# The second MoE's row blocks of one expert, taken two at a time through one split of the weights

## The chip, the cores and the metric

The program runs on one core of one Trainium2 chip. The metric is the device time of one execution in microseconds (us). The kernel before took 2382.6 us, the median of three runs from 2382.53 to 2384.66.

## The reference

An attention with a threshold on its scores feeds a dense mixture of experts (all 8 experts for every row, weighted by a gate that is normalised eight times over rows and columns). Its output x, 2304 rows of 512, goes into a second mixture in which each row is computed by one expert only. The change touches this last part alone:

```
logits = x @ w_gate
expert_idx = np.argmax(logits, axis=1)
...
gate_w = probs[np.arange(N), expert_idx]
for e in range(E):
    mask = expert_idx == e
    if not mask.any():
        continue
    xe = x[mask]
    h = np.maximum(xe @ w1[e], 0.0)
    ye = h @ w2[e]
    out[mask] = gate_w[mask, None] * ye
```

There are 8 experts; w1 is 512 x 1024 and w2 is 1024 x 512 for each.

## The kernel before

**Numbers in two halves.** Every large product is made with operands that are split into a rounded high half and a low half (the number less its high half). High by high, high by low and low by high give three products on TensorE in place of one. A split is a rounding copy, mostly on ScalarE, followed by a subtraction on VectorE or GpSimd (POOL in the profile).

**The stages.** Attention comes first, then the first MoE, whose first product is in line 567 and whose second is in line 583. When its last expert is done with two tiles of rows, these are routed: gate logits, the arg max, the probability, and the rank of each row within its expert. The second MoE, function `moe2`, follows.

**Slots.** The rows of one expert are cut into blocks of 128, and each block is a slot. The table function turns the counts per expert into a list of slots (expert, first rank), finds the rows of each slot by a small product (`ids`, line 1094) and the gate values (`gat`). This is done two times: after 14 of the 18 tiles, for the first KE = 6 slots, which take blocks that are already full, and after all tiles for the others. The first NU = 24 slots always run; the 25th runs in a branch if rows are left for it. The list is interleaved, so that the even slots walk through the experts in order, and the odd slots do the same.

**One slot.** Its 128 rows are gathered by an indirect DMA of POOL (`gath`, line 1150), transposed (`tx`, line 1156) and split. The expert's weights come in eight pieces of 128 x 1024: four of w1 (j = 0 to 3) and four of w2 (j = 4 to 7). Each piece is loaded by SyncE's queue (SP, line 1144) into a raw buffer, `xall` for even slots and `accs` for odd ones, and only if the expert differs from that of two slots before; otherwise the raw piece is still there. The split is done anew for every slot: the high half in line 1168 (`wsh`), the low half in line 1172 (`wsl`), into one of nine tiles `w` that go around as a ring. The first product (`g1`, line 1180) holds the rows stationary and moves the weights, 24 products of 512 columns into two banks. A ReLU (line 1187) takes the hidden rows to SBUF, eight transposes turn them (`th`, line 1192), lines 1197 and 1201 split them, and the second product (`g2`, line 1210) is again 24 products of 512 columns. ScalarE scales by the gate (`ys`, line 1216), and POOL scatters the rows to the output (line 1219).

**What sets the order.** Every engine works its instructions in the order in which they were written. That order comes from a list scheduler at build time (class `Sched`): each step is given an engine, a duration in us, a due time and the steps it needs, and resources that it takes and gives back (eight PSUM banks "b", nine weight tiles "w", and small pools "hh", "xs", "wr"). A slot's due time is `U0 + 1 + 2 * s`; a weight piece's place in the order of use is `pos(s, j)`, and its split is due 1.1 before that, its load 5 before. The second table's steps are put into the same plan, due at `U0 - 1.5`.

Of the kernel before, what the change touches and what calls it, by code (L numbers as in the profile page):

```python
# [10 lines left out]
F32 = mybir.dt.float32  # L11
# [11 lines left out]
class Sched:  # L23
# [18 lines left out]
    def run(self):  # L42
# [9 lines left out]
        ready = {e: [] for e in engs}      # (prio, i, ready_time)  # L52
# [6 lines left out]
        relq = []                          # (time, seq, op, own engine)  # L59
# [42 lines left out]
class Ring:  # L102
    """tiles handed out in the order in which they were given back"""
# [13 lines left out]
def attention(tc, sc, cst, dram, xT, q, k, v, tau, also=None):  # L117
# [11 lines left out]
    with ExitStack() as ctx:  # L129
        # first the tiles that the last pair is done with early: what comes after takes their place  # L130
# [190 lines left out]
        # the sums' reciprocals, from one per partition to one per column: turned, then spread over the partitions through DRAM  # L321
# [190 lines left out]
def moe1(tc, sc, cst, pools, xT, acc, wgs, w1, w2, NE=8, NW=9):  # L512
# [19 lines left out]
    # the first pieces are split by the engines that the attention leaves first  # L532
# [195 lines left out]
def out_row(i, hf):  # L728
    """first output row and row step of half tile hf of column tile i"""
# [3 lines left out]
TG = 2          # tiles routed together  # L733
TE = 14         # tiles that give the first slots
KE = 6          # slots that their full blocks fill
NU = 24         # slots that always run; the others run if rows are left for them


def moe2_setup(tc, cst, one, dram, w_gates, E=8, N=2304, NS=25):
    """constants and tables that no data goes into"""  # L740
# [37 lines left out]
def moe2_iota(tc, cst, r, E=8, NT=18, NS=25):  # L778
    nc = tc.nc
    nc.gpsimd.affine_select(out=r["lt"], in_=cst["ones"], pattern=[[1, 128]], compare_op=ALU.is_gt, fill=0.0, base=0, channel_multiplier=-1)  # L780
    nc.gpsimd.affine_select(out=r["tri"], in_=cst["ones"][:, 0:E * E].rearrange("p (a b) -> p a b", a=E), pattern=[[1, E], [-1, E]],
# [5 lines left out]
    # the blocks, in the order of their experts, go to the even slots first and then to the odd ones  # L787
    c = 128 + 2 * E
    for s0, n in ((0, KE // 2), (KE, (NU - KE) // 2)):
        nc.gpsimd.iota(it[:, c + s0:c + s0 + 2 * n].rearrange("p (a b) -> p a b", b=2), pattern=[[1, n], [n, 2]], base=0, channel_multiplier=0)  # L790
    nc.gpsimd.iota(it[:, c + NU:c + NS], pattern=[[1, NS - NU]], base=NU - KE, channel_multiplier=0)
    for i in range(NT):
        for hf in range(2):
            b, st = out_row(i, hf)
            c = 128 + 2 * E + NS + i
# [14 lines left out]
def moe2(tc, sc, cst, mt, pools, xall, accs, acc, w1, w2, out, elast, NS=25):  # L810
# [165 lines left out]
    def ohq(i):  # L976
        if i == 0:
            T["q"] = xs_p.tile([128, NT, 128], BF16, name="ohq", tag="xs")
# [43 lines left out]

# [1 line left out]
    ci = one.tile([128, 2, E], I32, name="ci")  # L1024
    cf = one.tile([128, 8, E], F32, name="cf")
    pr = one.tile([128, E, E], F32, name="pr")
    ge = one.tile([128, 2, NS, E], F32, name="ge")
    sl = one.tile([128, 4, NS], F32, name="sl")
    tab = one.tile([1, 2, NS], I32, name="tab")
    more = one.tile([1, 1], I32, name="more")  # L1030
    idi = one.tile([128, NS], I32, name="idi")
    idv = one.tile([128, 5, NS], F32, name="idv")
    gat = one.tile([128, NS], F32, name="gat")
    eq = one.tile([128, NT, NS - KE], BF16, name="eq")
    rhs = one.tile([128, NT, 5 * (NS - KE)], BF16, name="rhs")
    ful, cum, exc, ear, rem, dd = (cf[:, n] for n in range(6))
    erow, code, srow, tmp = (sl[:, n] for n in range(4))
    V_ = nc.vector

    def table(w, s0, s1, tiles, addc):  # L1040
        """the operations that make slots s0..s1 from the rows of the first `tiles` tiles, in order"""
        n = s1 - s0
        bs = lambda ap: ap.unsqueeze(1).to_broadcast([128, n, E])
        G0, G1 = ge[:, 0, 0:n], ge[:, 1, 0:n]
        it = mt["perm"][:, s0:s1]
        fin = w == 1
# [4 lines left out]
        L = [(P, .2, cnt, ["h"], []),  # L1051
             (V, .1, lambda: V_.tensor_scalar(ci[:, 0], T.pop(("cnt", w))[:, 0:E], addc, None, op0=ALU.add), [], ["h"]),
             (V, .1, lambda: V_.tensor_scalar(ci[:, 1], ci[:, 0], 7, None, op0=ALU.arith_shift_right), [], []),
             (V, .1, lambda: V_.tensor_copy(rem if fin else ful, ci[:, 1]), [], [])]
# [304 lines left out]
```

## Time and profile before

| what | value |
|---|---|
| median of 3 runs | 2382.6 us |
| span of the profiled execution | 2381.7 us |
| TensorE, matmuls (PE) | 2297.8 us busy, 96% |
| TensorE, weight loads (PEld) | 2052.2 us, 86% |
| VectorE (DVE) | 1059.0 us, 44% |
| ScalarE (ACT) | 824.0 us, 35% |
| GpSimd (POOL) | 828.3 us, 35% |
| first MoE, 400 to 1900 us | PE 1498.8 of 1500 us busy, DVE 322.3, ACT 312.4, POOL 317.1 |
| second MoE, 1987 to 2375 us | PE 332.2 of 388 us busy, DVE 366.1, ACT 216.2, POOL 244.6, granted clock 0.95 |

Shares over the whole span hide the stages. The second MoE is about a sixth of the time, and there VectorE is busy for 94% of the stretch, whereas it is busy for 21% of the first MoE's. A busy TensorE in such a table is not TensorE at its peak: a product that runs at a lower clock is counted as busy for longer. Engines other than TensorE cost time only where TensorE waits for them.

### The profile page before, as it was taken

Reading aid. Unit: us, or ns where it says so; the run is one execution under the profiler, and the core shown is the slowest. Engines: PE = TensorE matmul, PEld = TensorE weight load, DVE = VectorE, ACT = ScalarE, POOL = GpSimd, SP = SyncE. Lnnn points to the kernel's source line nnn. Section 1 sums busy time; section 2 is a strip of 40 time slices with the busy share of each in tenths; the row PEclk is TensorE's granted clock in tenths of the full one; section 3 lists DMA queues with packets and bytes.
Section 4 is the critical chain, followed back from the end, with each engine's and each line's share of the span. In section 5 each row is a group of like instructions: output and inputs, shape, how many; then the busy total and the mean of one; then the engine's idle time right before and its main releaser. Section 6 shows DMA issues by size and latency. Waiting matters only on the chain.

```text
span 2381.7 us, 32447 instructions
## 1 busy us (share of the span) xinstructions
PE 2297.8 (96%) x12379; PEld 2052.2 (86%) x12379; DVE 1059.0 (44%) x1944; ACT 824.0 (35%) x1466; POOL 828.3 (35%) x713
## 2 busy tenths in 40 slices
PE   7999999999999999999999999999999998788897
PEld 7999988888999999999999999999998887676675
DVE  8999972114221112211121112211122348999997
ACT  6888852122113112211211311221122124455564
POOL 6777752023214103211411401231041004566665
PEclk9999999999999999999999999999999999999999
DMA  3222120001002001100200200010011016343442
GB/s 91 61 62 62 38 92 28 1 18 54 1 1 71 1 1 36 36 1 1 71 1 1 65 7 1 18 54 1 1 36 27 14 45 256 107 154 116 170 153 86
DMA packets 98445, 121.25 MB, mean 51 GB/s; under 512 B 18830, under 2 KB 64030, under 8 KB 98272
## 3 DMA queue, kind: packets, MB, share of 16 engines
q1 hardware_dynamic: 94368, 109.71, 14.2%
q0 software_dynamic: 3920, 9.45, 1.1%
q8 instruction: 98, 1.61, 0.3%
q14 instruction: 59, 0.48, 0.1%
HBM read 164.92 MB, written 13.18 MB: 75 GB/s over the span
## 4 chain that ended last, share of the span: by engine, by line
PE 81%; DVE 10%; issue 4%; DMA 2%; ACT 2%; POOL 1%; SPq 0%; POOLq 0%; ACTq 0%; DVEq 0%
PE h L567 34%; PE y L583 33%; DVE w L1172 6%; PE pt_av L407 4%; PE s L282 3%; PE pt_m L350 2%; PE sy L1210 1%; DVE w L1168 1%; ACT w L1168 1%; DMA xall<-in_moe_w_dram 1%; POOL w L1172 1%; PE pt_k L251 1%; DVE hst L1201 1%; PE pt_av L410 1%; PE pt_q L241 0%
## 5 line engine op out<-in xcount | busy, mean ns | idle before, releaser
L567 PE MATMUL h<-xs,w 128*128 128x384 f32 x4608 | 871.1, 337 | 1.8 <-ACT w L539 1.0
L583 PE MATMUL y<-w,hh 128*128 128x512 f32 x3456 | 868.4, 395 | 3.7 <-ACT hh L572 2.3
L567 PEld LDWEIGHTS h<-xs,w 128*128 128x128 f32 x4608 | 819.1, 188 | 35.6 <-ACT w L539 1.4
L576 DVE SCALAR_TENSOR_TENSOR hh<-h,hh 128x384 fp32r<-128x384 f32 x384 | 214.2, 558 | 1211.3 <-ACT hh L572 1211.3
L583 PEld LDWEIGHTS y<-w,hh 128*128 128x128 f32 x3456 | 642.0, 188 | 120.6 <-ACT hh L572 2.8
L572 ACT ACTIVATE hh<-h 128x384 fp32r<-128x384 f32 x384 | 188.8, 492 | 1175.6 <-PE h L567 1153.0
L560 POOL TENSOR_TENSOR xs<-xall,xs 128x384 fp32r<-128x384 f32 x192 | 189.3, 1020 | 1114.6 <-ACT xs L539 1114.6
L1210 PE MATMUL sy<-w,hst 128*128 128x512 f32 x576 | 162.1, 427 | 42.7 <-DVE w L1172 40.2
L1210 PEld LDWEIGHTS sy<-w,hst 128*128 128x128 f32 x576 | 114.9, 204 | 76.0 <-DVE w L1172 48.6
L551 POOL TENSOR_TENSOR w<-wr,w 128x1024 fp32r<-128x1024 f32 x57 | 136.7, 2399 | 116.7 <-ACT w L539 113.2
L1180 PE MATMUL sh<-w,xst 128*128 128x512 f32 x576 | 150.7, 406 | 8.3 <-DVE w L1172 5.6
L407 PE MATMUL pt_av<-PTh,vsp 128*128 128x288 f32 x512 | 144.4, 323 | 0.0
L1180 PEld LDWEIGHTS sh<-w,xst 128*128 128x128 f32 x576 | 107.3, 193 | 38.0 <-DVE w L1172 12.1
L1172 DVE TENSOR_TENSOR w<-acc,w 128x1024 fp32r<-128x1024 f32 x60 | 128.6, 2155 | 10.8 <-ACT w L1168 10.4
L1172 DVE TENSOR_TENSOR w<-xall,w 128x1024 fp32r<-128x1024 f32 x60 | 127.5, 2136 | 9.2 <-ACT w L1168 8.9
L304 ACT ACTIVATE p<-s,stat 128x576 f32<-128x576 f32 x144 | 108.1, 752 | 30.7 <-DVE stat L287 30.5
L310 DVE SCALAR_TENSOR_TENSOR p<-s,stat,p 128x576 f32<-128x576 f32 x144 | 116.1, 809 | 4.9 <-ACT p L304 2.2
L287 DVE TENSOR_REDUCE stat<-s 128x1 f32<-128x576 f32 x144 | 108.2, 753 | 13.5 <-PE s L282 13.4
L282 PE MATMUL s<-kk,qst 128*128 128x288 f32 x512 | 96.7, 313 | 2.0 <-DVE p L310 1.8
L1172 POOL TENSOR_TENSOR w<-acc,w 128x1024 fp32r<-128x1024 f32 x36 | 92.8, 2584 | 16.5 <-ACT w L1168 15.7
L539 ACT CAST w<-wr 128x1024 fp32r<-128x1024 f32 x63 | 66.0, 1049 | 90.1 <-PE y L583 85.6
L1172 POOL TENSOR_TENSOR w<-xall,w 128x1024 fp32r<-128x1024 f32 x36 | 89.5, 2494 | 13.6 <-ACT w L1168 12.9
(222 smaller groups left out, 2079.1 us busy)
## 6 DMA issues: line engine op xcount, KB each, us to landing
xall<-in_moe_w_dram SPq DMA_DIRECT2D x104, 512.0 KB
acc<-in_moe_w_dram SPq DMA_DIRECT2D x96, 512.0 KB
wr<-in_moe_w_dram SPq DMA_DIRECT2D x128, 256.0 KB
kr<-in_k_dram SPq DMA_DIRECT2D x16, 256.0 KB
qr<-in_q_dram SPq DMA_DIRECT2D x16, 256.0 KB
vr<-in_v_dram SPq DMA_DIRECT2D x16, 256.0 KB
rbc<-rd SPq DMA_DIRECT2D x32, 128.0 KB
x1d<-acc SPq DMA_DIRECT2D x28, 128.0 KB
```

What stands on the lines that cost most here:

```text
L282: nc.tensor.matmul(ps[:, half, 0:288], lh, kk[p][:, h, s, half * 288:(half + 1) * 288], start=(i == 0 and s == 0), stop=(i == len(parts) - ...
L310: nc.vector.scalar_tensor_tensor(t, stile.pop(g)[:, :, 0:288], s[:, 1, j:j + 1], t, op0=ALU.is_ge, op1=ALU.mult, accum_out=s[:, 2, j:j + 1])
L407: nc.tensor.matmul(ps[:, 0:288], vv[:, h * 4 + kc, i, 64 - 64 * h:192 - 64 * h], mv[:, h, kc, c0:c1], start=(h == 0 and kc == 0 and n == 0 ...
L551: (nc.vector if WL(e, f) == V else nc.gpsimd).tensor_tensor(t[:, 1], wr[e, f], t[:, 0].bitcast(F32), op=ALU.subtract)
L560: nc.gpsimd.tensor_tensor(t[:, 1, k], xT[k][:, c * CH:(c + 1) * CH], t[:, 0, k].bitcast(F32), op=ALU.subtract)
L567: nc.tensor.matmul(ps[:, 0:CH], w[:, i, k * 128:(k + 1) * 128], x[:, j, k], start=(k == 0 and i + j == 0), stop=(k == NK - 1 and i == 1))
L572: nc.scalar.activation(hh[e, c, f][:, 0], hps[e, c, f][:, 0:CH], AF.Relu)
L576: nc.vector.scalar_tensor_tensor(t[:, 1], hps.pop((e, c, f))[:, 0:CH], 0.0, t[:, 0].bitcast(F32), op0=ALU.max, op1=ALU.subtract)
L583: nc.tensor.matmul(yps[e, c, t], h[:, i, t * 128:(t + 1) * 128], w[:, j, 512:1024], start=(f == 0 and i + j == 0), stop=(f == NF - 1 and i ...
L1172: eng.tensor_tensor(t[:, 1], rawp(s, j), t[:, 0].bitcast(F32), op=ALU.subtract)
L1180: nc.tensor.matmul(T["h", s][hf], x[:, i, k * 128:(k + 1) * 128], w[:, j, hf * 512:(hf + 1) * 512], start=(k == 0 and i + j == 0), stop=(k ...
L1210: nc.tensor.matmul(T["y", s], h[:, i, f * 128:(f + 1) * 128], w[:, j, r * 512:(r + 1) * 512], start=(f == 0 and i + j == 0), stop=(f == 7 ...
```

## The change

**Units in place of slots.** The list now has units. A pair is 256 rows of one expert, a single is 128. Three pairs come from the early table (KP = 3), then seven pairs (NP = 7) and four singles (NS = 4) always run, in the order MAIN, in which a single stands after each of the pairs with the numbers 4 to 7. Five more pairs (NR = 5, the units REST) run in a branch if rows are left for them.

```
+TG = 2
+TE = 14
+KP = 3
+NP = 7
+NS = 4
+NR = 5
+MAIN = [0, 1, 2, 3, 4, 10, 5, 11, 6, 12, 7, 13, 8, 9]
...
+def half(s, h):
...
+    return 2 * s + h - max(0, min(s - KP - NP, NS))
```

**Weights.** Each unit, pair or single, loads and splits its eight pieces once, and the load no longer depends on the expert of the unit before. All high halves are ScalarE's (six of eight were), all low halves VectorE's (five of eight were, the pieces 1, 4 and 7 were POOL's).

```
     def ld_w(s, j):
-        nc.sync.dma_start(out=rawv(s, j), in_=wsrc(j, bass.ds(T["e", s], 1)), cond=(T["c", s] != 0), cond_hint=False)
+        nc.sync.dma_start(out=rawv(s, j), in_=wsrc(j, bass.ds(T["e", s], 1)))
...
-    def wsl(s, j, eng):
+        nc.scalar.copy(T["w", s, j][:, 0], rawp(s, j))
+
+    def wsl(s, j):
         t = T["w", s, j]
-        eng.tensor_tensor(t[:, 1], rawp(s, j), t[:, 0].bitcast(F32), op=ALU.subtract)
+        nc.vector.tensor_tensor(t[:, 1], rawp(s, j), t[:, 0].bitcast(F32), op=ALU.subtract)
```

**A pair's products.** Two gathers and two sets of transposes fill one tile of 4 x 256 columns. In the first product (`q1`) the weights are held and the rows move: 256 columns a product, 96 products a pair, into four banks. The hidden values come out turned already, so `prh` (ReLU and rounding, ScalarE) and `prl` (ReLU and subtraction, VectorE) split them straight from PSUM, and no transposes follow. The second product (`q2`) is 48 products of 512 columns, 24 for each half of the rows. Singles keep `g1`, `th` and `g2`.

```
+    def q1(s, k, b):
+        if k == 0:
+            T["hp", s, b] = bank(f"hp{s}_{b}")
+        x, w, ps = T["xs", s], T["w", s, k], T["hp", s, b]
+        for r in range(2):
+            f = 2 * b + r
+            for i, j in SPL:
+                nc.tensor.matmul(ps[:, r * 256:(r + 1) * 256], w[:, i, f * 128:(f + 1) * 128], x[:, j, k * 256:(k + 1) * 256],
+                                 start=(k + r + i + j == 0), stop=(k == 3 and i == 1), skip_group_check=True)
...
+    def prl(s, b):
+        t = T["hh", s, b]
+        nc.vector.scalar_tensor_tensor(t[:, 1], T.pop(("hp", s, b)), 0.0, t[:, 0].bitcast(F32), op0=ALU.max, op1=ALU.subtract)
+
+    def q2(s, b, r, h):
...
+        t, w = T["hh", s, b], T["w", s, 4 + b]
+        c = r * 256 + h * 128
+        for i, j in SPL:
+            nc.tensor.matmul(T["y", s, h], t[:, i, c:c + 128], w[:, j, r * 512:(r + 1) * 512],
+                             start=(b + r + i + j == 0), stop=(b == 3 and r == 1 and i == 1))
```

**The plan.** A unit's place is `at[s]`, which grows by 2 for a single and 4 for a pair; as before, a piece is loaded when the unit two places earlier in the order has split its own.

```
-        """place of a weight piece in the order of use, 4 to a phase of 5 us"""
-        return U0 + 1 + 2 * s + .25 * j if j < 4 else U0 + 4 + 2 * s + .25 * (j - 4)
+        n = len(hs_of(s))
+        return at[s] + .25 * n * j
...
-            op(("wh2", s, j), V if hi_v else A, .6 if hi_v else .95, pu - 1.1, partial(wsh, s, j, hi_v), [("rwin", s, j), ("wh2",) + prevp if prevp else first], acq=["w"])
-            op(("wl2", s, j), G if lo_g else V, 2.36 if lo_g else 1.13, pu - 1.1, partial(wsl, s, j, nc.gpsimd if lo_g else nc.vector), [("wh2", s, j)])
+            op(("wh2", s, j), A, 1.05, pu - 1.1, partial(wsh, s, j), [("rwin", s, j), ("wh2",) + prevp if prevp else first], acq=["w"])
+            op(("wl2", s, j), V, 1.25, pu - 1.1, partial(wsl, s, j), [("wh2", s, j)])
```

**The tables** deal out pairs first and singles behind them; the comparison of every row with every slot (`EQ`, and the five products `R` of it) grows in the second table from 18 x 19 to 18 x 28 elements a partition, and is written into the tile `ohq`, which the pool "xs" gets back after the index product.

**The order on VectorE around the second table.** Before, the bulk operations of the table (line 1098) stood between the roundings and subtractions of two slots. `w` is a weight tile of the ring, `hst3` the split hidden rows of slot 3, `rhs` the table's operand:

```order
L1085 CAST tab_5095<-sl_5094 1x19
L1097 TENSOR_TENSOR eq_5100<-sl_5094,gf_5088 128x342
L1098 TENSOR_TENSOR rhs_5101<-eq_5100,idp_82 128x18x19
L1172 TENSOR_TENSOR w4_5062<-xall_69,w4_5062 128x1024
L1098 TENSOR_TENSOR rhs_5101<-eq_5100,idp_82 128x18x19
L1168 CAST w5_5063<-xall_69 128x1024
L1098 TENSOR_TENSOR rhs_5101<-eq_5100,gp_5086 128x18x19
L1201 TENSOR_TENSOR hst3_17266<-th3_0_17130,hst3_17266 128x512
```

Now they stand together, and behind the index products (`ids1`) four subtractions of the fourth unit's weights (line 1227, out of the raw buffer `acc`) come ahead of the third pair's first hidden half (`hp2_0`, line 1250):

```order
L1146 TENSOR_TENSOR ohq_16181<-ohq_16181,gp_5086 128x18x28 x3
L1227 TENSOR_TENSOR w0_5058<-acc0_5067,w0_5058 128x1024
L1150 COPY idv_5100<-ids1_17250 128x5x28
L1151 SCALAR_TENSOR_TENSOR idt_5099<-idv_5100 128x28
L1152 TENSOR_SCALAR idt_5099<-idt_5099 128x28
L1153 SCALAR_TENSOR_TENSOR idi_5098<-idt_5099 128x28
L1154 TENSOR_TENSOR gat_5101<-idv_5100 128x28
L1227 TENSOR_TENSOR w6_5064<-acc1_5068,w6_5064 128x1024
L1155 TENSOR_TENSOR gat_5101<-gat_5101,idv_5100 128x28
L1227 TENSOR_TENSOR w7_5065<-acc2_5069,w7_5065 128x1024
L1227 TENSOR_TENSOR w2_5060<-acc3_5070,w2_5060 128x1024
L1250 SCALAR_TENSOR_TENSOR hp2_0_17346<-hp2_0_17138,hp2_0_17346 128x512
```

In line 1250's row the destination and the first operand are the tile of the hidden half and the PSUM bank, both called `hp2_0`.

**The order on TensorE.** Before, in the middle of the stage, one slot's second product (`sy8`) filled the time in which the next slot's hidden rows were rounded and turned (`th9`):

```order
L1180 MATMUL sh9_1_18106<-w1_5059,xst9_18033 128x512
L1210 MATMUL sy8_18160<-w7_5065,hst8_18083 128x512 x6
L1210 MATMUL sy8_18160<-w0_5058,hst8_18083 128x512 x6
L1192 MATMUL th9_0_18181<-ident_62,hr9_18167 128x128 x4
L1192 MATMUL th9_1_18187<-ident_62,hr9_18167 128x128 x4
L1210 MATMUL sy8_18160<-w3_5061,hst8_18083 128x512 x6
```

Now a single (unit 10) has the next pair's first products (`hp5`) at that place:

```order
L1270 MATMUL sh10_1_17958<-w6_5064,xst10_17924 128x512
L1239 MATMUL hp5_0_18025<-xst5_18004,w4_5062 128x256 x6
L1282 MATMUL th10_0_18033<-ident_62,hr10_18022 128x128 x4
L1239 MATMUL hp5_1_18039<-xst5_18004,w4_5062 128x256 x6
L1282 MATMUL th10_1_18050<-ident_62,hr10_18022 128x128 x4
L1239 MATMUL hp5_2_18055<-xst5_18004,w4_5062 128x256 x6
L1239 MATMUL hp5_3_18065<-xst5_18004,w4_5062 128x256 x6
L1300 MATMUL sy10_18073<-w7_5065,hst10_18048 128x512 x6
```

Between the two products of a pair (here unit 4, `hp4` and `py4`) stands only the transposing of the next unit's rows, where a slot before had its own transposes:

```order
L1239 MATMUL hp4_2_17773<-xst4_17679,w7_5065 128x256 x6
L1239 MATMUL hp4_3_17781<-xst4_17679,w7_5065 128x256 x6
L1208 MATMUL tx10_0_17877<-ident_62,xall_69 128x128 x4
L1258 MATMUL py4_0_17884<-w2_5060,hp4_0_17856 128x512 x3
L1258 MATMUL py4_1_17892<-w2_5060,hp4_0_17856 128x512 x3
```

So the banks `hp4_0` to `hp4_3` are filled in the order in which the second product takes them, and the first of them is complete three groups of six before the last.

More of the change, by code (lines that the diff above doesn't have):

```diff
@@ L1031, in moe2 @@
[L1031 to L1037, printed above, removed]
-    V_ = nc.vector
[L1040 to L1044, printed above, removed]
+    ci = one.tile([128, 2, 2 * E], I32, name="ci")
@@ new lines, in moe2, with table @@
+    gat = one.tile([128, NH], F32, name="gat")
+    num, cum, exc, dd, vv, bb = (cf[:, n] for n in range(6))
+    ear = cf[:, 6, 0:E]
+    mm = cf[:, 7, 0:1]
+    erow, code, srow, unit = (sl[:, n] for n in range(4))
+    V_ = nc.vector
+    def table(w):
+        s0, s1 = (KP, NT_) if w else (0, KP)
+        h0, h1 = (2 * KP, NH) if w else (0, 2 * KP)
+        S = 2 * E if w else E
+        tiles = NT if w else TE
+        n, m = s1 - s0, h1 - h0
+        bs = lambda ap: ap[:, 0:S].unsqueeze(1).to_broadcast([128, n, S])
+        G0, G1 = ge[:, 0, 0:n, 0:S], ge[:, 1, 0:n, 0:S]
@@ L1107, in table @@
-        return L, nreg
+                nc.tensor.matmul(ps[:, 0:5 * m], T["q"][:, i], T["rhs"][:, i, 0:5 * m], start=(i == 0), stop=(i == tiles - 1))
+        neq = len(L)
+        big = .06 + .00105 * tiles * m
+        v(lambda: V_.tensor_tensor(EQ(), ch[:, h0:h1].unsqueeze(1).to_broadcast([128, tiles, m]), b2(gf), op=ALU.is_equal), big)
+        for a in range(5):
+            v(lambda a=a: V_.tensor_tensor(R()[:, :, a], EQ(), b2(mt["idp"][:, a] if a < 2 else gp[:, a - 2]), op=ALU.mult), big)
@@ L1223, in moe2 @@
     xdone = [("xl", elast, 5, k) for k in range(4)] + [("xh", elast, 5, k) for k in range(4)]
+    order = MAIN + REST
+    turn = {s: n for n, s in enumerate(order)}
+    hs_of = lambda s: range(1 if single(s) else 2)
+    at, u = {}, U0 + 1
+    for s in order:
+        at[s] = u
+        u += 2 * len(hs_of(s))
+    uend = at[REST[0]]
     for i in range(2):
@@ L1275, in moe2 @@
-    splits(op, range(NU), ("lg1", TE // TG - 1))
-    for s in range(NU):
+        u = at[s]
+        one_ = single(s)
+        for h in hs_of(s):
+            op(("tx", s, h), P, .44, u - 1.6, partial(tx, s, h), [("gain", s, h)], acq=["b"])
+            op(("txh", s, h), A, .6, u - 1.6, partial(txh, s, h), [("tx", s, h)] + ([("txh", s, 0)] if h else []), acq=["hh" if one_ else "xs"] if h == 0 else [])
+            op(("txl", s, h), V, .6, u - 1.6, partial(txl, s, h), [("txh", s, h)], rel=["b"])
@@ L1277, in moe2 @@
+        for h in hs_of(s):
+            op(("ys", s, h), A, .7, u + 1, partial(ys, s, h), [last[h]], acq=["wr"], rel=["b"])
+            op(("sca", s, h), G, 1.2, u + 1, partial(scao, s, h), [("ys", s, h)])
+            op(("scao", s, h), "DMA", .8, u + 3.3, lambda: None, [("sca", s, h)], rel=["wr"])
+    splits(op, MAIN, ("lg1", TE // TG - 1))
+    for s in MAIN:
+        loads(op, s)
         slot(op, s)
@@ L1288, in rest @@
                 s2.res(nm, n)
-            splits(s2.op, range(NU, NS), None)
-            for s in range(NU, NS):
+            splits(s2.op, REST, None)
+            for s in REST:
+                loads(s2.op, s)
                 slot(s2.op, s)
```

320 lines of the change are left out of this document (188 added, 132 removed).

## The prediction

> **What bounds the kernel now.** I read the windows first, to find the stage that the change touches, then who waits for whom in it, then the groups of instructions, and last the timeline of one stretch. The second MoE's slots run from about 1987 us to the end. A window from the middle of them, with its columns (stretch, length, busy us of PE, PEld, DVE, ACT, POOL, the granted clock, DMA share, GB/s):
>
> ```profile
> 2180.00:2240.00 60.00, 51.21 (x234) 40.34 (x232) 57.76 (x38) 36.40 (x48) 41.24 (x20) 0.97 0.56 195
> ```
>
> VectorE is busy for 57.8 of 60 us there, ScalarE for 36.4, and the DMA engines for 56%. TensorE's 51.2 also counts slowed products. What TensorE waited for from 1950 us on (total, times, longest):
>
> ```profile
> PE sy L1210 <- DVE w L1172: 40.2, 24, 3.9
> PE sh L1180 <- DVE w L1172: 5.6, 8, 1.6
> ```
>
> The wait is for one line, the low half of a weight piece. The groups (count, then busy us and mean ns):
>
> ```profile
> L1172 DVE TENSOR_TENSOR w<-acc,w 128x1024 fp32r<-128x1024 f32 x60 | 128.6, 2155 | 10.8 <-ACT w L1168 10.4
> L1172 DVE TENSOR_TENSOR w<-xall,w 128x1024 fp32r<-128x1024 f32 x60 | 127.5, 2136 | 9.2 <-ACT w L1168 8.9
> L1172 POOL TENSOR_TENSOR w<-acc,w 128x1024 fp32r<-128x1024 f32 x36 | 92.8, 2584 | 16.5 <-ACT w L1168 15.7
> L1168 ACT CAST w<-acc 128x1024 fp32r<-128x1024 f32 x72 | 74.1, 1050 | 3.4 <-DMA acc<-in_moe_w_dram 3.4
> L1201 DVE TENSOR_TENSOR hst<-th,hst 128x512 fp32r<-128x512 f32 x48 | 32.5, 680 | 0.5 <-ACT hst L1197 0.5
> L1150 POOL DMA_INDIRECT xall<-x1d,idi x25 | 39.2, 1567 | 82.1 <-DVE gat L1106 62.5 <-PE tx L1156 16.0 <-issue 2.2
> ```
>
> A subtraction means 2.15 us on VectorE. The timeline shows why (start, length, engine):
>
> ```profile
> 2324.93 1.23 DVE L1172 TENSOR_TENSOR w<-acc,w 128x1024 fp32r<-128x1024 f32 x1
> ...
> 2325.83 2.60 POOL L1172 TENSOR_TENSOR w<-xall,w 128x1024 fp32r<-128x1024 f32 x1
> 2326.08 3.43 DVE L1172 TENSOR_TENSOR w<-xall,w 128x1024 fp32r<-128x1024 f32 x1
> ```
>
> Alone it takes 1.23 us; begun under POOL's subtraction it ends 1.1 us after that one (2329.51 against 2328.43). It stood still until POOL was done. So GpSimd's share of the split costs VectorE about what it saves, and VectorE (5 subtractions at 2.15, two roundings, three 0.68s: 14.6 us a slot) sets the pace above TensorE's own work.
>
> **TensorE's own work.** Back-to-back rates from the chain of waits in stretches where TensorE never stops (start, length, count):
>
> ```profile
> 1905.17 2.10 PE h L567 x12
> 1907.27 2.08 PE y L583 x9
> 1913.54 1.75 PE x1t L857 x16
> 1918.09 0.91 PE l1t L875 x8
> ```
> ```profile
> 150.08 0.64 PE pt_k L251 x8
> 160.86 1.60 PE pt_av L407 x12
> ```
>
> That is 0.231 us for a product of 512 columns, 0.175 for 384, 0.133 for 288, 0.114 for 256 with 16 columns of weights, 0.080 for 128, and 0.109 for an fp32 transpose. A slot has 48 products of 512 and 12 transposes: 11.09 + 1.31 = 12.4 us, and 24 slots 297.6 us. The stage lasts from
>
> ```profile
> 1987.26 0.60 PE L1156 MATMUL tx<-ident,xall 128*128 128x128 f32 x4
> ```
> to the end of
> ```profile
> 2372.74 1.43 PE L1210 MATMUL sy<-w,hst 128*128 128x512 f32 x5 [0.40 <-POOL w L1172]
> ```
>
> 386.9 us. Routing and tables inside it take about 6.0 (16 transposes 1.75, two gate groups 1.82, the rest an estimate from rows of their kind). So **386.9 - 297.6 - 6.0 = 83.3 us are lost**: 46 are the two waits above, some 7 are smaller ones, and about 30 are products at a reduced clock, as here after a wait:
>
> ```profile
> 2080.00:2084.00 4.00, 0.61 (x2) 0.51 (x3) 4.00 (x2) 0.91 (x2) 2.25 (x1) 0.85 0.95 341
> 2084.00:2088.00 4.00, 4.00 (x11) 3.14 (x10) 3.96 (x6) 0.00 (x0) 0.00 (x0) 0.50 0.99 380
> ```
>
> The Trainium skill's page "TensorE: Matmul & The Clock Gate" (section "HAM oscillation — how this bites in real kernels") says that idle gaps beyond some 3.4 us bring the half clock back. The 0.50 after a window that was nearly all idle agrees; by that rule the 30 us go as soon as no wait is that long, and if they stayed, the sum below would be 2328.
>
> **The change, part by part.** Counting rows per expert in the reference (292, 134, 1263, 394, 46, 1, 18, 156) gives 24 blocks before. With 1792 rows known early, three full pairs of one expert exist; seven pairs and four single blocks are left, exactly what always runs. So there are 10 pairs and 4 singles.
>
> *First product.* In a pair it is 96 products of 256 columns with 128 columns of weights, a form that the trace does not show. It lies between 0.114 (same width, fewer weight columns) and 0.133 (wider); a line through the 128 and 288 rows gives 0.122, which I take. Pair: 96 x 0.122 + 48 x 0.231 + 8 x 0.109 = 23.7 us against 24.8 for two slots; the hidden rows' transposes go. In all 236.7 + 49.6 = 286.3 us: **-11.3**, with bounds -19 and -1.
>
> The same page (section "LDWEIGHTS (loading the stationary operand)") gives columns/1.2, so 107 ns for 128 columns. By it the load still fits under 256 columns; unhidden, 960 products would cost 103 us more, and the sum would be 2400. The 128-column row at 0.080, below 107, speaks against the figure.
>
> *Splits.* 14 units have 112 pieces instead of 192, each 1.05 us of ScalarE and one subtraction of VectorE. The two prices of a subtraction with POOL elsewhere are the 1.23 above and this row of the chain, which counts from one start to the next:
>
> ```profile
> 2009.80 1.13 DVE w L1172
> ```
>
> I take 1.13 to 1.23, since POOL keeps only indirect DMAs; the other end is 2.15. A pair needs VectorE for 8 x 1.13 + 6 x 0.65 = 13 us of 23.7, a single for 8 x 1.13 + 3 x 0.65 = 11 of 12.4; ScalarE needs 8 x 1.05 for the pieces, 0.6 for each of a pair's six and a single's five other roundings, and 0.7 for each scaled output: 13.4 and 12.1. Singles stand between pairs, so each cycle of 36.1 us holds 24 of VectorE and 25.5 of ScalarE, and the nine weight tiles let the splits run eight pieces ahead. With this cover the 83.3 us go; at 2.15 a cycle needs 40 us of VectorE, and four cycles lose 16.
>
> *Loads.* Every unit loads its 4.2 MB: 14 loads, where the slots' experts by the same count made 12. A busy window moved
>
> ```profile
> 1988.00:1992.00 4.00, 4.00 (x27) 3.52 (x26) 3.70 (x4) 3.37 (x6) 3.42 (x2) 1.00 1.04 398
> ```
> 398 GB/s, so a unit takes 10.5 us, under each 12.4 or 23.7. Two raw buffers give a load a whole unit of time. Cost 0, except once, next.
>
> *The second table.* It grows to some 45 small operations (about 0.18 each), and its bulk ones from 342 to 504 elements:
>
> ```profile
> 2055.92 0.50 DVE L1098 TENSOR_TENSOR rhs<-eq,gp 128x342 bf16<-128x342 bf16 x1
> ```
> so 0.67 each. From the first pair's product to the index products VectorE has 20 subtractions (22.6), 16 half-size subtractions (10), 87 small ones (15.7), 9 bulk ones (5.3) and 1.1 of comparisons: 54.7 us. TensorE comes there after two pairs (47.4), routing (2.6) and nine groups of six (6.6): 56.6 us after its first product at 1989.1, at 2045.7. I take 1 us of wait (bounds 0 and 10, a quarter of the small ones' gaps). Behind it VectorE's order puts the fourth unit's first four subtractions ahead of the third pair's hidden halves (hp2), and that unit's loads wait for the table. What a table cost the first time:
>
> ```profile
> 1970.32 0.16 DVE L1085 CAST tab<-sl 1x6 int32<-1x6 f32 x1
> ...
> 1976.85 1.05 ACT L1168 CAST w<-xall 128x1024 fp32r<-128x1024 f32 x1 [3.36 <-DMA xall<-in_moe_w_dram]
> ...
> 1980.48 1.04 ACT L1168 CAST w<-xall 128x1024 fp32r<-128x1024 f32 x1 [0.39 <-DMA xall<-in_moe_w_dram]
> ```
>
> 6.4 us from the table to the first rounding, then 3.6 for two more pieces. The table stands at about 2041, so the fourth piece is subtracted at about 2054.6 and the first hidden half done at 2055.5; TensorE wants it at 2052.6. **3 us** (bounds 0 and 12). With 0.7 at the first pair, the early waits are 4.7.
>
> *Within units.* From a pair's first to its second product stands a ReLU rounding of 512 columns, like this group, and a subtraction like L1201's (0.68):
>
> ```profile
> L1187 ACT ACTIVATE hr<-sh 128x512 f32<-128x512 f32 x48 | 28.4, 598 | 39.9 <-PE sh L1180 39.9
> ```
>
> Together 1.3 us. The first bank is done three groups of six (2.2 us) before the last, so I take 0.2 us a pair for what else may be late, an estimate: 2.0 in all. In a single, roundings of the next pair's pieces stand between the two ReLUs: 0.6 each, 2.4. At the end a second scatter follows: 0.5.
>
> **Sum:** -11.3 - 83.3 + 4.7 + 2.0 + 2.4 + 0.5 = **-85.0**. It is made against the profiled execution:
>
> ```profile
> span 2381.7 us, 32447 instructions
> ```
>
> The median run, 2382.6, is 0.9 above that: 2296.7 of span, **2297.6** of time.
>
> **Rivals.** (1) The waits are 15 to 30 us larger: the table chain is in order on a VectorE with 2 us to spare, and each late operation delays the index products, the gathers and the loads behind them: 2312 to 2328. For it stands a row of the same view of waits, at the index products:
>
> ```profile
> PE ids L1094 <- DVE rhs L1098: 2.3, 1, 2.3
> ```
>
> Against it: POOL no longer stops VectorE. (2) VectorE still stands still under POOL's DMA work (mean 1567 ns a gather): 16 + 20 early subtractions x 1 us = 36, 2333; here the change would not do what it says. Against it, this subtraction kept its 1.22 us while a scatter was issued (timeline):
>
> ```profile
> 2048.14 1.22 DVE L1172 TENSOR_TENSOR w<-xall,w 128x1024 fp32r<-128x1024 f32 x1
> 2048.41 1.84 POOL L1219 DMA_INDIRECT out_dram<-ys,idi  x1 [0.67 <-DVE tab L1080]
> ```
> (3) The first product is paced by its weight loads at the length in their records,
>
> ```profile
> L567 PEld LDWEIGHTS h<-xs,w 128*128 128x128 f32 x4608 | 819.1, 188 | 35.6 <-ACT w L539 1.4
> ```
> 188 ns: 960 x 0.066 = 63, 2361. Against it, that same load ran under 0.175 and, in the 128 rows, 0.080. (4) Slower than before: a fifth single block or an eighth late pair. Then the branch runs five more pairs, 5 x 23.7 = 118, and their first load cannot start before it (6.4 and a gather): about 2425. It decides at one block; 134 rows of one expert are 6 above a block's edge, 394 of another 10.
>
> **How the numbers follow.** The forecast with its bounds, 2282 to 2312: 0.70. Rival 1: 0.15. Rival 2: 0.05. Rival 3: 0.06. Rival 4: 0.03. Below 2282: 0.01. The range runs to rival 1's end, 2282 to 2328, 0.85. A measurement here tells about 0.2% (4.8 us) from no change. Faster by more: 0.96, the same 0.01, slower 0.03.
>
> **What would show it.** Right: L1227 on VectorE at about 1.2 us with 112 executed, no subtraction on POOL in this stage, a group of six 256-column products at 0.73, a pair and a single in 36 us, TensorE over 95% busy at clock 1.0 after 2070, waits for the stage near 9 us, 24 scatters, last product near 2289. Wrong: L1227 near 2 us (rival 2), groups of six at 0.8 or more (rival 3), a gap of over 10 us at the index products or at the fourth unit (rival 1), more than 24 scatters (rival 4). A queue that I took as covered, such as roundings that wait for a weight tile while ReLUs stand behind them on ScalarE, would show as waits of every unit, not of one.

## The result and the profile after

| | before | after |
|---|---|---|
| median time | 2382.57 us (2382.01 to 2384.66, 4 runs) | 2293.61 us (2292.15 to 2293.86, 4 runs) |
| span of the profiled execution | 2381.7 us | 2290.4 us |

The ratio is 0.9619, with a 95% interval from 0.9606 to 0.9633: 89.0 us less, where 85.0 were forecast. The page of after, its first line and the busy times of the engines (us, share of the span, instructions):

```profile
span 2290.4 us, 31977 instructions
PE 2254.2 (98%) x12699; PEld 2048.7 (89%) x12699; DVE 887.6 (39%) x1904; ACT 780.0 (34%) x1394; POOL 634.5 (28%) x641
```

Two windows of after, the stretch of the early pairs and that of the pairs and singles behind them (columns as in the prediction):

```profile
1985.00:2045.00 60.00, 59.76 (x423) 54.69 (x422) 51.77 (x140) 33.15 (x46) 8.09 (x7) 1.00 0.65 236
2085.00:2275.00 190.00, 190.00 (x1150) 169.35 (x1150) 117.79 (x120) 114.50 (x143) 32.97 (x28) 1.00 0.58 190
```

TensorE is now busy for 190 of 190 us at the full clock, and VectorE for 62%. In the window from the middle of before it was 51 of 60, with VectorE at 96%. The groups show the subtraction alone with VectorE, and the new product with its weight load (count, busy us, mean ns, idle before):

```profile
L1227 DVE TENSOR_TENSOR w<-acc,w 128x1024 fp32r<-128x1024 f32 x56 | 68.4, 1223 | 36.3 <-ACT w L1223 35.5
L1227 DVE TENSOR_TENSOR w<-xall,w 128x1024 fp32r<-128x1024 f32 x56 | 67.8, 1223 | 30.0 <-ACT w L1223 29.2
L1239 PE MATMUL hp<-xst,w 128*128 128x256 f32 x960 | 121.6, 284 | 0.2 <-DVE xst L1219 0.2
L1239 PEld LDWEIGHTS hp<-xst,w 128*128 128x128 f32 x960 | 117.7, 191 | 2.6 <-DVE xst L1219 1.6
```

A subtraction takes 1.22 us, where it was 2.15 on average. What TensorE still waited for from 2030 us on (total, times, longest):

```profile
PE tx L1208 <- DMA xall<-x1d,idi: 1.9, 1, 1.9
PE py L1258 <- ACT hp L1246: 0.9, 1, 0.9
PE py L1258 <- DVE hp L1250: 0.6, 1, 0.6
```

The two waits of `py` stand in the third pair's second product, that of `tx` at the transposes of the fourth unit's rows. The chain of after gives the rates (start, length, count), and with them TensorE's own work:

```profile
2065.46 11.51 PE hp L1239 x96
2100.79 10.92 PE py L1258 x48
2122.04 5.47 PE sy L1300 x24
```

A 256-column product takes 0.120 us (0.122 was priced), a 512-column one 0.2276 (0.231). With eight transposes at 0.109 a pair is 11.51 + 10.92 + 0.87 = 23.30 us and a single 48 x 0.2276 + 12 x 0.109 = 12.23.

**A yardstick.** The part ahead of the change varies: the count product named below starts between 1963.9 and 1968.2 us in the profiled executions. So the stage is measured from the first count product (`cnt`, 14 tiles) to the end of the span. The row of it in the timeline of before, and then of after:

```profile
1964.30 0.18 PE L1050 MATMUL cnt<-ohs,onesb 128*128 128x8 bf16 x1
```
```profile
1964.00 0.18 PE L1079 MATMUL cnt<-ohs,onesb 128*128 128x8 bf16 x1
```

That is 2381.7 - 1964.3 = 417.4 us before and 2290.4 - 1964.0 = 326.4 after, 91.0 less. All profiled executions in this measure, one of each kernel:

| kernel | median us | stage us |
|---|---|---|
| before | 2382.6 | 417.4 |
| slots_new_split | 2317.2 | 348.6 |
| pairs_old_split | 2320.6 | 354.2 |
| after | 2293.6 | 326.4 |
| early_new_late_old | 2306.8 | 337.7 |
| singles_last | 2297.3 | 327.3 |
| tail_halves | 2292.0 | 325.0 |
| tail_halves_2 | 2291.6 | 323.6 |
| hidden_first | 2290.6 | 322.5 |
| loads_behind_gather | 2293.5 | 327.3 |
| second_half_loads_behind_gather | 2293.3 | 326.2 |
| loads_held | 2291.0 | 323.6 |
| order_and_tail | 2286.6 | 319.5 |

How far the stage of one kernel varies between executions was not measured. after and the two versions whose edit missed its aim (loads_behind_gather, second_half_loads_behind_gather) lie between 326.2 and 327.3 us, so a difference of about 1 us is not read here.

### The profile page after: what moved, and what is told of

It is laid out like the page before. It is cut to its first block, busy times and chain, and to the rows that moved or that the text cites. A ratio compares the mean times of both kernels' runs of the same rounds, so it can differ in the third digit from the quotient of the medians.

```text
span 2290.4 us, 31977 instructions
## 1 busy us (share of the span) xinstructions
PE 2254.2 (98%) x12699; PEld 2048.7 (89%) x12699; DVE 887.6 (39%) x1904; ACT 780.0 (34%) x1394; POOL 634.5 (28%) x641
## 4 chain that ended last, share of the span: by engine, by line
PE 93%; issue 2%; DVE 2%; DMA 2%; ACT 1%; SPq 0%; POOL 0%; POOLq 0%; ACTq 0%; DVEq 0%
PE h L567 35%; PE y L583 35%; PE pt_av L407 4%; PE s L282 4%; PE py L1258 4%; PE hp L1239 4%; PE pt_m L350 2%; PE sh L1270 1%; PE pt_k L251 1%; PE sy L1300 1%; PE pt_av L410 1%; DMA out_dram<-ys,idi 0%; PE pt_q L241 0%; PE tx L1208 0%; PE lt L598 0%
## 5 line engine op out<-in xcount | busy, mean ns | idle before, releaser
L1239 PE MATMUL hp<-xst,w 128*128 128x256 f32 x960 | 121.6, 284 | 0.2 <-DVE xst L1219 0.2
L1239 PEld LDWEIGHTS hp<-xst,w 128*128 128x128 f32 x960 | 117.7, 191 | 2.6 <-DVE xst L1219 1.6
L1258 PE MATMUL py<-w,hp 128*128 128x512 f32 x480 | 113.1, 393 | 1.6 <-ACT hp L1246 0.9
L1258 PEld LDWEIGHTS py<-w,hp 128*128 128x128 f32 x480 | 88.9, 188 | 20.2 <-ACT hp L1246 1.2
L407 PEld LDWEIGHTS pt_av<-PTh,vsp 128*128 128x128 f32 x512 | 91.8, 188 | 1.5
L691 DVE SCALAR_TENSOR_TENSOR acc<-y,Pm,acc 128x512 f32<-128x512 f32 x126 | 86.5, 743 | 0.8 <-POOL acc L687 0.8
L539 ACT CAST xs<-xall 128x384 fp32r<-128x384 f32 x192 | 84.7, 511 | 0.0
L366 POOL TENSOR_TENSOR PTl<-rp,PTh 128x512 fp32r<-128x512 f32 x64 | 82.5, 1289 | 4.3
```

The source lines that it names most:

```text
L407: nc.tensor.matmul(ps[:, 0:288], vv[:, h * 4 + kc, i, 64 - 64 * h:192 - 64 * h], mv[:, h, kc, c0:c1], start=(h == 0 and kc == 0 and n == 0 ...
L539: nc.scalar.copy(out, in_)
L1239: nc.tensor.matmul(ps[:, r * 256:(r + 1) * 256], w[:, i, f * 128:(f + 1) * 128], x[:, j, k * 256:(k + 1) * 256], start=(k + r + i + j == 0 ...
L1258: nc.tensor.matmul(T["y", s, h], t[:, i, c:c + 128], w[:, j, r * 512:(r + 1) * 512], start=(b + r + i + j == 0), stop=(b == 3 and r == 1 a ...
```

## The experiments

**The two halves of the change, each alone.** The first takes before, with its 24 slots, and gives it only the new division of the split:

```
-            hi_v, lo_g = j in (3, 6), j in (1, 4, 7)
+            hi_v, lo_g = False, False
```

with the plan's costs of after (1.05 and 1.25).

> The 24 slots of before, with only the division of the split changed: all high halves on ScalarE, all low halves on VectorE. Theory (POOL's subtractions hold VectorE up): a subtraction falls from 2.15 to about 1.23 us, VectorE then needs 8 x 1.23 + 3 x 0.68 = 11.9 us a slot against TensorE's 12.2 to 12.4, and most of the loss goes except around the second table, where VectorE has some 98 us of work in TensorE's 82: 2315 to 2340. Rival (the number of splits is what counts, 2.15 us is what a subtraction costs): VectorE needs 8 x 2.15 + 2 = 19 us a slot and the kernel is slower than before, about 2450.

Measured: 2317.18 us (2314.27 to 2317.33), ratio 0.9723 (0.9708 to 0.9738), as forecast. Its groups of subtractions, the stretch around the second table, and a stretch of plain slots:

```profile
L1172 DVE TENSOR_TENSOR w<-acc,w 128x1024 fp32r<-128x1024 f32 x96 | 112.6, 1216 | 0.0
L1172 DVE TENSOR_TENSOR w<-xall,w 128x1024 fp32r<-128x1024 f32 x92 | 108.0, 1216 | 1.3 <-ACT w L1168 1.3
```
```profile
2055.00:2085.00 30.00, 20.77 (x95) 15.28 (x94) 24.51 (x32) 15.76 (x19) 7.16 (x5) 0.89 0.61 211
2185.00:2285.00 100.00, 100.00 (x492) 83.36 (x492) 88.69 (x89) 90.20 (x114) 26.00 (x15) 1.00 0.48 174
```

VectorE does three subtractions more in each slot and two roundings fewer, and is less busy than before: 89% in place of 96%. The same instruction on the same tiles goes from 2155 and 2136 ns on average to 1216 once POOL subtracts nothing. The trace of before shows the same split within one kernel: 51 of its 120 subtractions on VectorE ran with none of POOL's beside them and took 1.21 to 1.23 us, and the 69 with one beside them took 2.83 us on average, up to 5.61. The plain slots run without a gap; what is lost is lost around the second table. The rival, by which 2.15 us is the price of a subtraction, is out. The profiled execution is the fastest of the four; by the medians the gain is 65 us. No run separates the end of the stalls from the two roundings (46.4 us of VectorE over the stage of before), which left VectorE with the same edit.

The second takes after and gives it the old division:

```
-            op(("wh2", s, j), A, 1.05, ..., partial(wsh, s, j), ...
-            op(("wl2", s, j), V, 1.25, ..., partial(wsl, s, j), ...
+            hi_v, lo_g = j in (3, 6), j in (1, 4, 7)
+            op(("wh2", s, j), V if hi_v else A, .6 if hi_v else .95, ..., partial(wsh, s, j, hi_v), ...
+            op(("wl2", s, j), G if lo_g else V, 2.36 if lo_g else 1.13, ..., partial(wsl, s, j, nc.gpsimd if lo_g else nc.vector), ...
```

> The units of after, with the division of the split of before: pieces 3 and 6 rounded on VectorE, pieces 1, 4 and 7 subtracted on POOL. Theory: subtractions on VectorE go back to about 2.1 us, but a cycle of a pair and a single needs 30.5 us of VectorE in 35.5, so only the stretch up to the index products, 62 us of VectorE in TensorE's 56, loses: 3 to 12 us more than after, 2297 to 2306. Rival (POOL's stalls cost as much with pairs as with slots): 30 us more or worse, 2323.

Measured: 2320.64 us (2320.33 to 2320.85), ratio 0.9737 (0.9723 to 0.9752): 27 us above after. The expectation of 3 to 12 was wrong, and the rival nearer. TensorE's waits in it, a group of small routing operations, and a subtraction in the timeline with what POOL did beside it:

```profile
PE py L1258 <- DVE hp L1250: 13.6, 7, 5.3
PE rk L961 <- DVE oha L926: 5.2, 2, 5.0
```
```profile
L989 DVE TENSOR_TENSOR gf<-rs 128x2 f32<-128x2 f32 x2 | 4.5, 2251 | 0.0
```
```profile
2145.57 6.14 DVE L1227 TENSOR_TENSOR w<-xall,w 128x1024 fp32r<-128x1024 f32 x1
2145.84 4.77 POOL L1227 TENSOR_TENSOR w<-xall,w 128x1024 fp32r<-128x1024 f32 x2
```

Two things were left out of that expectation. POOL holds up not only VectorE's subtractions but also operations on two numbers a partition (the two of this group stood beside a subtraction of POOL's and took 2.25 us on average; in after they take 0.15 and 0.16), so a chain of routing steps is stretched as a whole. And one subtraction can stand still through two of POOL's in a row (6.14 us, and so in three more places); the hidden halves of a pair stand behind it in VectorE's order, however much VectorE idles later. Half an engine's time free does not cover a delay at the point of use. The two longest waits, 5.0 and 5.3 us, were also followed by products at half the clock: the granted clock was 0.50 from 2002 to 2006 us and from 2040 to 2044.

The two alone save 68.8 and 63.2 us of the stage, together 91.0. They do not add up, since either removes most of the same wait.

**Where the old division hurts.** Only the first three pairs keep the new division:

```
+            hi_v, lo_g = j in (3, 6) and s >= KP, j in (1, 4, 7) and s >= KP
```

> The units of after; the first three pairs keep the new division of the split, the units from the fourth on get that of before (pieces 3 and 6 rounded on VectorE, 1, 4 and 7 subtracted on POOL). Theory: of the 27 us that the old division cost with pairs, two thirds came from the stretch up to the index products, where small routing operations of VectorE stand behind held-up subtractions; the rest, 2.2 us in each cycle of a pair and a single, stays: 8 to 11 us above after, 2302 to 2305, and 334 to 338 us from the first count product to the end of the span (326.4 in after). Rival (the loss is that of all units alike): more than 20 us stay, above 2313.

Measured: 2306.79 us (2304.71 to 2311.5), and 337.7 us of stage: 11.3 above after, in the forecast of 334 to 338, though the median is 2 us above its own. The later units wait much as in the run before, where six of the seven waits, 8.3 us in all, are theirs:

```profile
PE py L1258 <- DVE hp L1250: 10.9, 7, 2.0
```

So of the 27.8 us of stage that the old division costs with pairs, 16.5 come from the stretch with the routing and 11.3 from the later units.

**Singles between the pairs.**

```
-MAIN = [0, 1, 2, 3, 4, 10, 5, 11, 6, 12, 7, 13, 8, 9]
+MAIN = [0, 1, 2, 3, 4, 5, 6, 7, 8, 9, 10, 11, 12, 13]
```

> After, with the four singles run back to back at the end in place of one after each of four pairs. Theory of the prediction (a cover of pairs is what carries the singles): a single needs 12.1 us of ScalarE and 11.9 of VectorE in TensorE's 12.2, with the splits at most eight pieces ahead, so some 3 to 10 us of waits come in; the last unit has one scatter in place of two (about 4 us less), and its hidden rows' rounding and turning lie bare (about 2.5 more): 2294 to 2304. Rival (the place of the singles does not matter): 2290 to 2293.

Measured: 2297.31 us (2293.32 to 2299.58), but its stage is 327.3 us, 0.9 above after; the rest of the difference lies ahead of the count product (1968.2 in this execution). From 2085 to 2285 us TensorE is nearly full:

```profile
2085.00:2285.00 200.00, 196.80 (x1180) 174.17 (x1178) 120.07 (x123) 117.27 (x148) 32.59 (x30) 1.00 0.60 189
```

Of its waits none is for a split of weights; the longest, 2.5 us, is for a gather. So the mechanism of the theory, that the splits need the pairs as cover, falls, as slots_new_split shows too, where units of one block follow each other at 100 of 100. But the rival, by which the place of the singles does not matter, is not borne out either: the end behind the last product is 3.1 us shorter here (9.5 in place of 12.6, the last unit has one scatter), so about 4 us are lost ahead of it, and the waits for gathers grow from 2.8 to 5.6. The time itself lies in the theory's range of 2294 to 2304.

**The end.** In after, the last scatter waits for the one before it (timeline: last products, then the two scatters):

```profile
2266.69 11.07 PE L1258 MATMUL py<-w,hp 128*128 128x512 f32 x48
2278.08 0.98 POOL L1311 DMA_INDIRECT out_dram<-ys,idi  x1 [17.91 <-ACT ys L1307]
2282.05 0.98 POOL L1311 DMA_INDIRECT out_dram<-ys,idi  x1 [2.99 <-DMA out_dram<-ys,idi]
```

From the last product (2277.76) to the end of the span are 12.6 us, against 2381.7 - 2374.2 = 7.5 before. The order of the last pair's second product was changed, so that one half of its rows is done earlier; (b, h) is the hidden bank and the half of the rows:

```
+            q2s = [(b, r, h) for b in range(4) for r in range(2) for h in range(2)]
+            if s == MAIN[-1]:
+                q2s = [(b, r, h) for b, h in ((0, 0), (1, 0), (2, 0), (0, 1), (3, 0), (1, 1), (2, 1), (3, 1)) for r in range(2)]
```

> After, with only the order of the last pair's second product changed: the first half of the rows gets all its products 4.1 us before the second half. Theory: of the 12.6 us between the last product and the end of the span, the wait of the second scatter for the first one's landing (2.99 us) goes, 3 to 4 us less: 2289.6 to 2290.6. Rival (the tail is fixed cost at the end of the program, or the scatters' transfers collide whatever the order): 2293 to 2294.

Measured: 2292.0 us (2291.38 to 2294.01), 1.4 above the upper end of the forecast, stage 325.0. The last product now lies 9.7 us ahead of the end, 3 us less, but TensorE waited 1.2 us for a fourth hidden tile, of which there are three. The times overlap those of after, and 1.4 us of stage is little; the 3 us at the end are read in the profile. So the next order gives one back sooner:

```
-... for b, h in ((0, 0), (1, 0), (2, 0), (0, 1), (3, 0), (1, 1), (2, 1), (3, 1)) ...
+... for b, h in ((0, 0), (1, 0), (0, 1), (2, 0), (3, 0), (1, 1), (2, 1), (3, 1)) ...
```

> As tail_halves, with the order chosen so that a tile for the last hidden bank comes free in time (its first half's last product stands 4.1 us before the end as there). Theory: the 1.2 us that TensorE waited there for a hidden tile go and the 3 us of the tail stay gone: 322 to 323 us from the first count product to the end (326.4 in after, 325.0 in tail_halves). Rival (the last scatter's own transfer sets the end, so that an earlier first one gains nothing more): 325.

Measured: 2291.55 us (2290.42 to 2293.68), stage 323.6, 0.6 above the forecast's upper end but 2.8 below after; the times still overlap. The end of it, where the second scatter starts as soon as its rows are scaled:

```profile
2277.13 0.98 POOL L1311 DMA_INDIRECT out_dram<-ys,idi  x1 [14.52 <-ACT ys L1307]
2277.78 2.43 PE L1258 MATMUL py<-w,hp 128*128 128x512 f32 x10
...
2280.25 0.69 ACT L1307 ACTIVATE ys<-py,gat 128x512 f32<-128x512 f32 x1 [3.39 <-PE py L1258]
2281.21 0.98 POOL L1311 DMA_INDIRECT out_dram<-ys,idi  x1 [3.10 <-ACTq L1414]
```

**The third pair.** After's timeline at the place of the three waits:

```profile
2049.82 1.23 DVE L1227 TENSOR_TENSOR w<-acc,w 128x1024 fp32r<-128x1024 f32 x1 [0.21 <-ACT w L1223]
2050.33 0.73 PE L1258 MATMUL py<-w,hp 128*128 128x512 f32 x2 [0.95 <-ACT hp L1246]
2050.96 1.88 DVE L1250 SCALAR_TENSOR_TENSOR hp<-hp,hp 128x512 fp32r<-128x512 f32 x3
2051.70 2.57 PE L1258 MATMUL py<-w,hp 128*128 128x512 f32 x10 [0.63 <-DVE hp L1250]
...
2056.63 0.63 PE L1208 MATMUL tx<-ident,xall 128*128 128x128 f32 x4 [1.93 <-DMA xall<-x1d,idi]
```

A subtraction of the fourth unit (L1227) stands ahead of the hidden halves, as the order shown with the change had it, and on ScalarE a rounding of that unit (L1223, 1.05 us from 2048.73) stands ahead of the hidden halves' ReLU (L1246), for which the first of the waits is. Two orders were changed, in one run, so their shares are not separated:

```
-            op(("tx", s, h), ..., [("gain", s, h)], acq=["b"])
+            op(("tx", s, h), ..., [("gain", s, h)] + ([("q2", KP - 1, 2, 1, 1)] if s == KP else []), acq=["b"])
...
-            op(("wh2", s, j), ..., [("rwin", s, j), ("wh2",) + prevp if prevp else first], acq=["w"])
+            op(("wh2", s, j), ..., [("rwin", s, j), ("wh2",) + prevp if prevp else first] + ([("prl", KP - 1, j - 1)] if s == KP and 1 <= j < 5 else []), acq=["w"])
```

> After, with two changes of order at the third and fourth unit: the fourth unit's second to fifth weight pieces are rounded behind the third pair's hidden banks, and its rows are turned after three quarters of the third pair's second product, not after one. Theory: the two waits at the third pair's second product (0.95 and 0.63 us) and the 1.93 us for the gather go: 2290, 322.5 to 323.5 us from the first count product to the end. Rival (the waits only move: the fourth unit's first product then waits for its own pieces or rows): 325 to 328 us, no change in the time.

Measured: 2290.59 us (2289.05 to 2291.86), stage 322.5, as forecast. From 2030 us on one wait is left:

```profile
PE hp L1239 <- DVE xst L1219: 0.2, 1, 0.2
```

**The late gather.** Is the 1.93 us wait that of a gather behind weights? The fourth unit's gathers took 6.6 and 7.5 us to land in after. First only the plan was changed:

```
-            op(("rw", s, j), ..., [("regs", s)] + pd)
+            op(("rw", s, j), ..., [("regs", s)] + pd + ([("tx", KP, 1)] if s == KP + 1 else []))
```

> After, with the fifth unit's weight loads held back until the fourth unit's rows have been turned. Theory (the fourth unit's gathers, issued at 2047.4 and 2049.0, land late since 4.2 MB of weights share the DMA engines with them): they land within 4 us of their issue and the wait of 1.93 us goes; the loads start 10 us later and are still in time: 324 to 325 us from the first count product to the end (326.4 in after). Rival (an indirect gather takes 6 us in any case, 6.4 was the median): the wait stays, 326 to 327; or the late loads make the fifth unit wait, more than 328.

Measured: 2293.48 us (2293.0 to 2294.65), stage 327.3, gathers 6.5 us. A step that the plan names moves only the place in SyncE's queue. The fifth unit's loads now started at 2056.8 us in place of 2045.9, but five other loads moved up ahead of them, the fourth unit's own eight stood in front as before, and the DMA engines went on at 405 GB/s from 2048 to 2052 us. So this told nothing of the question, and neither did the next, in which the fourth unit's pieces 4 to 7 were put back in the same way:

```
-... if s == KP + 1 else []))
+... if s == KP + 1 or (s == KP and j >= 4) else []))
```

> After, with the fourth unit's last four weight pieces and all of the fifth unit's held back until the fourth unit's rows have been turned, so that only the fourth unit's first four pieces (2.1 MB, 5.3 us at 398 GB/s, issued before the gathers) can lie in front of its gathers. Theory (weights in flight make the gathers late): they land within 5 us of their issue (6.3 to 7.5 in after, 3.7 to 4.5 where the DMA engines were a third busy) and TensorE's wait for them at the transposes goes. What else moves on ScalarE and VectorE is not kept, so the time may be 2290 to 2296. Rival (the landing time is that of a gather behind other POOL work and does not depend on the weights): 6 us or more, and a wait of 1 to 2 us.

Measured: 2293.28 us (2291.63 to 2294.48), stage 326.2, gathers 5.7 to 7.4 us, wait 2.1. A real hold needs a read of the gathered rows in SyncE's queue:

```
+    def hold():
+        nc.sync.dma_start(out=mt["x1b"][0, 0:1, 0:16], in_=xr[1][0:1, 0:16])
...
-... if s == KP + 1 else []))
+... [("hold", 0)] if KP < s < REST[0] or (s == KP and j >= 4) else []))
```

> After, with a copy of 64 bytes out of the gathered rows put into SyncE's queue ahead of the fourth unit's last four weight pieces and of all later loads, so that these really start only when the fourth unit's gathers have landed (in the two runs before only their place in the queue was changed, and the traces show the loads running on). Theory (weights in flight make the gathers late): with the DMA engines idle, they land within 4 us of their issue (6.3 to 7.5 in after), and the wait of about 2 us at the transposes goes; 324 to 325 us from the first count product to the end (326.4 in after), if the loads that start some 6 us later are in time. Rival (the landing time does not depend on the weights): 6 us and a wait of 2 us as before, 326 or more.

Measured: 2291.04 us (2290.51 to 2292.68), stage 323.6, where 324 to 325 was forecast. The time from issue to landing of the fourth unit's gathers, in after and then in this kernel:

```profile
DMA to landing us min/median/max: 6.6/7.0/7.5
```
```profile
DMA to landing us min/median/max: 3.7/3.7/3.7
```

The eight transposes then run in one piece without a wait. In the same kernel the fifth unit's two gathers, issued at 2057.6 and 2058.9 us among the held loads, took 7.5 and 6.9 us to land. With only the fourth unit's first four pieces loaded ahead of them the gathers land 3 us sooner, and the fifth unit's loads, which start about 10 us later in the stage, are still in time.

**Both together.** The two diffs of hidden_first and the two of tail_halves and tail_halves_2 in one kernel:

> After, with the order of hidden_first and the last pair's order of tail_halves_2 together. Theory (the two places lie apart and add up): 326.4 - 3.9 - 2.8 = 319.7 us from the first count product to the end of the span, and a time of 2287 to 2289, below both kernels. Rival (the two interact, or the gain of hidden_first's run was chance in the gathers): 322 us or more, above 2290.

Measured: 2286.61 us (2286.26 to 2287.48), ratio to before 0.9595 (0.9582 to 0.9608), stage 319.5 where 319.7 was forecast. This is the fastest of the versions, below both kernels; the two repairs add up.

## Why the prediction was right

- **The bound.** VectorE, held up by POOL's subtractions, set the pace: shown by slots_new_split, where only the division changed and 68.8 us of the stage went (two roundings a slot left VectorE with it, whose share is open). The page of after alone could not have told this from the smaller number of splits. The Trainium skill ("SBUF — State Buffer", section "SBUF: two separate sides") says that a VectorE operation with two SBUF inputs and a GpSimd operation that reads SBUF take the same ports in turn, each for a whole instruction, and the runs agree: 1.22 us alone, and beside a subtraction of POOL's typically until 1.09 us past its end. Indirect DMAs of POOL held none up: 30 of after's 112 subtractions ran beside one, and the longest took 1.27 us.
- **TensorE's own work.** The term of -11.3 held: 24 x 12.233 = 293.6 before and 10 x 23.302 + 4 x 12.233 = 282.0 after, 11.6 less. Both levels lie 4 us lower than priced: a 512-column product takes 0.2276 us where a row of nine had given 0.231, and in a pair a 256-column one 0.120 where 0.122 was taken; so 87 us, not 83, had been lost, and nearly all of it went.
- **The 128-column weight load** stays hidden: its record is 191 ns, about the length on which rival 3 rested, but 96 products take 11.51 us, 0.120 each. The Trainium skill ("TensorE: Matmul & The Clock Gate", section "LDWEIGHTS (loading the stationary operand)") gives a load in ns as its columns divided by 1.2, so an estimate of 107 ns for 128 columns. That fits under the product, and the pace agrees with a load beside it.
- **The clock.** The slowed products went with the waits: the granted clock is 1.00 in both windows of after. The term was too large: a granted clock of 0.95 over the 388 us of the stage before is worth some 19 us (an estimate, 0.05 x 388), and what the rest of the "about 30" was, no view names. The Trainium skill's rule on gaps beyond some 3.4 us ("TensorE: Matmul & The Clock Gate", section "HAM oscillation — how this bites in real kernels") does not fit the trace of before: of nine stretches at half the clock between 1980 us and the last product, one follows a gap above 3.4 us (3.87), and eight follow gaps of 2.3 to 3.1. One of these in its timeline, eleven products that take 2.5 us at the full clock:

```profile
2348.84 4.38 PE L1210 MATMUL sy<-w,hst 128*128 128x512 f32 x11 [2.53 <-DVE w L1172]
```

- **Early waits.** The sum of 4.7 was right by luck, since its parts were not. No wait came at the index products (1 was taken), and 1.6 at the hidden halves (3 was taken); 1.9 came at the gather, which had been priced at nothing with the loads ("Cost 0, except once"). loads_held shows that weights in flight were its cause.
- **Within units.** 2.0 for the pairs and 2.4 for the singles were priced; from 2085 to 2275 us TensorE is busy for 190 of 190, and a cycle of a pair and a single takes 35.8 us where its own work is 35.5. The first bank's rounding and subtraction fit under three groups of six, and the next pair's first products cover the single's ReLUs.
- **The end.** "At the end a second scatter follows: 0.5" was the term that was mis-sized most: 12.6 - 7.5 = 5.1 us. The second scatter waits for the first one to land before it is issued; tail_halves and tail_halves_2 took 3 us of it away.

Against the forecast of 85.0 the stage gave 91.0, 6 more. Own work and what had been lost before gave 4.3 more. Between the first transposes and the last product 6.9 us are left over beside the own work and the prediction's 6.0 for the routing, where 4.7 + 4.4 had been priced: 2.2 more. An earlier start gave 4.1 more: the first transposes came 18.9 us after the count product, where it had been 23.0 before (18.7 in slots_new_split, so this is the division's, not the pairs'). The end took 4.6 of it back. So the nearness of the total is in part luck: the last product, forecast near 2289, ended at 2277.8, 11 us sooner, and the longer end hid part of it.

Of the rivals, larger early waits (1) did not come, with VectorE busy for 51.8 of 60 us in that stretch, and POOL's DMA work (2) did not hold VectorE up. One argument of the prediction was not needed: that the splits of singles are carried by the pairs around them; no wait for a split came without it.

## What to carry to other kernels

If a group's mean on one engine is well above its shortest records, look in the timeline for what runs on the other engine at the same moment before counting instructions; work given to a second engine may save nothing if it stops the first. Two repairs of the same wait do not add up, so test each alone before keeping both. When an engine becomes the bound, read the last microseconds and the first use of each gathered block: what is left is order, not work.

## What had not been expected of the hardware

- A subtraction of 1.22 us lasted 6.14 us beside two of POOL's, though its record begins 0.27 us before the first of them (four such in pairs_old_split); and an operation on two numbers a partition 2.25 us on average (pairs_old_split).
- In loads_behind_gather TensorE waited 2.0 us and soon after 0.62 us, and then ran at half speed, 10 products in 4.64 us where 2.3 are usual. The timeline, and the windows with the granted clock (the third number from the end):

```profile
2052.53 0.74 PE L1258 MATMUL py<-w,hp 128*128 128x512 f32 x2 [2.00 <-ACT hp L1246]
2053.90 4.64 PE L1258 MATMUL py<-w,hp 128*128 128x512 f32 x10 [0.62 <-DVE hp L1250]
```
```profile
2052.00:2056.00 4.00, 2.84 (x7) 2.03 (x8) 3.98 (x5) 2.39 (x4) 0.00 (x0) 0.64 1.05 398
2056.00:2060.00 4.00, 4.00 (x15) 3.34 (x14) 0.86 (x2) 1.17 (x3) 0.34 (x1) 0.51 1.03 410
```

The first of the two waits was enough: the granted clock is 1.00 from 2052.53 to 2053.10 us and 0.50 from 2053.20 on, ahead of the second wait, which began at 2053.28. A wait of 1.97 us was followed by the half clock too (early_new_late_old, 0.50 from 2053.6 to 2056.9). But in after 0.95, 0.63 and 1.93 us left the clock at 1.00, and so did 2.50 in singles_last and 2.8 twice in before. So the length of one gap does not decide it; what does, these runs do not show.
